# Sums placed where their exps end, keys loaded two gate steps sooner, last projection in column halves: sliding-window attention with a gated feed-forward block on one core

## The chip, the cores and the metric

The kernel runs on one core of a Trainium2 chip. The metric is the time of one execution in device microseconds. Every comparison below uses executions of the state "fast". The span of the trace is some 1.9 us shorter than that time (335.7 against 337.54 us in the profiled run of the kernel before); stretches of the trace are given in us from the start of the span.

Short names: PE is the tensor engine, DVE the vector engine, ACT the scalar engine, POOL and SP the two others. POOL, ACT and SP issue the transfers (DMA; POOLq, ACTq and SPq in the traces). PSUM is where the kernel keeps the tiles that PE writes (`o_ps`, `s_ps` and the like in the traces). In the traces `qT` and `kT` are the turned queries and keys, `xT` the output of the attention, `sg` the silu of a gate, `hT` the output of the gate steps and `wo` the output weights. A warming matmul is one whose result nobody reads. The fifth block of a projection is `c = 4`, the first that needs the second third of the output weights.

## The reference, cut to what matters

```python
def _attn_ref(q, k, v):                       # 8 batches, 8 heads, 576 rows, 64 columns
    scores = np.matmul(q, k.transpose(0, 1, 3, 2)) / np.sqrt(D)
    mask = (rel >= 0) & (rel < 64)            # rel = query row - key row
    attn = softmax(np.where(mask, scores, -1e9))
    return np.matmul(attn, v)

def _moe_ref(x, w_gate, w_val, w_out):        # x: 4608 x 512; 512 -> 1536 -> 512
    g = x @ w_gate
    return (g * sigmoid(g) * (x @ w_val)) @ w_out
```

The kernel cuts the 4608 rows into nine tiles of 512. A tile has four pairs of heads (scores, exp, sums of the exps, values), then twelve gate steps of eight 512-column matmuls, then a projection in four slices of twelve.

## The kernel before

The warming of PE at the start, while the first loads are under way:

```python
    nc.vector.memset(ones[:], 1.0)
    ...
    def keep_warm(n):
        for _ in range(n):
            nc.tensor.matmul(warm[0:D], ones[:, 0:D], ones[:])
    keep_warm(7)
```

The end of the first tile's attention. `totals` is the pair of matmuls for a pair's sums; the logarithm and an exp of its negative make the inverse.

```python
    def log_of(u):
        d_ps = one("d_ps")
        totals(0, u, d_ps)
        inverse[0, u] = room(1)[:, 0]
        log(inverse[0, u], d_ps)

    keep_warm(6)
    for u in range(2):
        values(0, u, ...)
    log_of(2)
    pairs = [gate_tiles() for _ in range(2)]
    gate_part(0, (0,), pairs, 0)
    log_of(3)
    gate_part(0, (1,), pairs[1:], 0)
    for u in (2, 3):
        invert(inverse[0, u])
    values(0, 2, one("ao_ps"))
    ...
```

The first tile's gate steps load and turn the second batch's keys, then turn its queries (a DVE transpose of data that POOL's queue loads):

```python
    for m in range(12):
        ...                                          # gate step m
        if 3 <= m < 7:                               # load two heads' keys, issued by ACT
            hs = slice(2 * m - 6, 2 * m - 4)
            load_runs(nc.scalar, raw_k[:, hs], k, 1, hs)
        if 7 <= m < 11:                              # cast them on ACT
            u = m - 7
            join(on_a, keys[:, u], raw_k[:, 2 * u:2 * u + 2])
        if m >= 8:                                   # transpose on PE, copy out on DVE
            u = m - 8
            ...
            split_k(kT[1][:, u, :], tp[:])
        if m >= 10:
            turn_q(1, m - 10)
    turn_q(1, 2)
    turn_q(1, 3)

    halves = out_tile(), out_tile()
    for u in range(4):
        scores(1, u)
        if u % 2:                                    # output weights: blocks 0-5, then 6-11
            project_part(0, (0, 1), halves, range(3 * u - 3, 3 * u + 3))
```

POOL's queue brings, in this order: the gate and value weights in ten transfers, the queries of batch 1 in four, the output weights in thirds of four blocks (`weights_o(0, 4)`, `(4, 8)`, `(8, 12)`), then v of batch 1. The last projection is four times `project`: twelve matmuls of 512 columns, one copy, four stores of 64 KB.

The softmax here doesn't subtract the row's maximum and nothing guards it: scores larger than these inputs give would overflow.

## Time and profile before

| | before |
|---|---|
| time, three runs | 337.47 us median (337.40 to 337.78) |
| span; PE busy | 335.7 us; 323.2 us (96%) |
| PE idle 21.3 to 42 us | 1.78 us |
| second batch's first gate matmul | 56.29 us |
| start of the last copy, and from there to the end | 331.26; 4.44 us |

How to read it: PE is the bound. Only its waits, and work that stands alone at the two ends, can be saved. The lines are in the prediction.

### The profile page before, as it was taken

The numbers are of one execution on the slowest core, as the hardware profiler recorded it, in microseconds if no ns is written. First come the engines' busy times: TensorE is split into PE (matmuls) and PEld (weight loads), VectorE is DVE, ScalarE is ACT, GpSimd is POOL, SyncE is SP. The second block draws the span as 40 slices with busy tenths as digits, with TensorE's granted clock in tenths as the row PEclk, the third lists the DMA queues.
The fourth block names the chain that finished last, engine by engine and source line by source line (L and its number), as shares of the span: only waits on it lengthen the run. The fifth ranks groups of instructions, "written<-read, shape, count | busy, mean of one in ns | idle before, by whom it ended". The sixth has DMA issues, their size and how long they took to land.

```text
span 335.7 us, 6932 instructions
## 1 busy us (share of the span) xinstructions
PE 323.2 (96%) x2683; PEld 153.9 (46%) x2729; DVE 214.2 (64%) x318; ACT 169.2 (50%) x241; POOL 137.8 (41%) x247
## 2 busy tenths in 40 slices
PE   8899799999999999999999999999999999999994
PEld 3444344444544454445444544444444444544441
DVE  5754766588667756785678656865786476753431
ACT  4764656336733763366435553565347633763300
POOL 5944345946767965256123896163200000000000
PEclk9999999999999999999999999999999999999999
DMA  7999999999899499639931999199401320010013
GB/s 261 205 202 226 229 188 223 125 205 215 147 248 186 52 176 234 124 58 209 185 89 20 170 180 167 12 189 177 111 0 48 79 56 3 23 72 31 3 32 94
DMA packets 83057, 44.12 MB, mean 131 GB/s; under 512 B 63824, under 2 KB 77648, under 8 KB 83024
## 3 DMA queue, kind: packets, MB, share of 16 engines
q0 software_dynamic: 49328, 22.56, 54.2%
q1 hardware_dynamic: 31680, 19.02, 20.6%
q10 hardware_dynamic: 2016, 2.10, 2.2%
q8 instruction: 21, 0.34, 0.4%
q14 instruction: 12, 0.10, 0.1%
HBM read 54.00 MB, written 9.44 MB: 189 GB/s over the span
## 4 chain that ended last, share of the span: by engine, by line
PE 88%; DMA 6%; DVE 3%; issue 2%; ACT 1%; DVEq 0%
PE g_ps L306 26%; PE v_ps L306 26%; PE o_ps L315 25%; PE s_ps L227 3%; DMA k_f<-in_k_dram 3%; PE ao_ps L271 3%; PE d_ps L245 3%; DMA q_f<-in_q_dram 1%; PE tp L174 1%; PE g_ps L286 1%; ACT E L233 1%; DVE kT L177 1%; PE v_ps L286 1%; DMA out_dram<-os__4409 1%; DMA out_dram<-os__4428 1%
## 5 line engine op out<-in xcount | busy, mean ns | idle before, releaser
L299 ACT ACTIVATE sg<-g_ps 128x512 f32<-128x512 f32 x108 | 64.4, 597 | 112.1 <-PE g_ps L306 79.9
L300 DVE TENSOR_TENSOR hT<-sg,v_ps 128x512 bf16<-128x512 f32 x108 | 74.9, 694 | 62.9 <-PE v_ps L306 59.9
L306 PE MATMUL v_ps<-xT,wv 128*128 128x512 bf16 x417 | 108.3, 379 | 0.5
L306 PE MATMUL g_ps<-xT,wg 128*128 128x512 bf16 x413 | 107.6, 379 | 0.5
L315 PE MATMUL o_ps<-wo,hT 128*128 128x512 bf16 x405 | 96.5, 380 | 1.6 <-issue 0.6
L107 POOL DMA_DIRECT2D k_s<-in_k_dram x112 | 60.7, 551 | 29.8 <-DMA q_s<-in_q_dram 20.5
L306 PEld LDWEIGHTS <-wv 128*128 128x128 bf16 x424 | 41.5, 98 | 50.0
L306 PEld LDWEIGHTS <-wg 128*128 128x128 bf16 x424 | 41.4, 98 | 49.5 <-issue 0.3
L315 PEld LDWEIGHTS <-hT 128*128 128x128 bf16 x432 | 39.6, 98 | 45.1 <-issue 0.4
L233 ACT ACTIVATE E<-s_ps 128x1024 bf16<-128x1024 f32 x36 | 35.2, 1021 | 8.4 <-PE s_ps L227 8.2
L277 DVE TENSOR_TENSOR xT<-ao_ps,r 128x512 bf16<-128x512 f32 x36 | 24.7, 691 | 22.7 <-ACT r L256 20.5
L196 DVE STREAM_TRANSPOSE kT<-k_s 128x512 bf16<-128x512 bf16 x28 | 35.9, 1284 | 0.0
L253 ACT ACTIVATE r<-d_ps 128x512 f32<-128x512 f32 (+1 forms) x35 | 21.0, 601 | 22.4 <-PE d_ps L245 22.4
L235 DVE TENSOR_TENSOR E<-E,mask 128x1024 bf16<-128x1024 bf16 x28 | 20.5, 739 | 11.5 <-ACT E L233 11.5
L87 POOL DMA_DIRECT2D q_s<-in_q_dram x28 | 15.3, 558 | 26.7 <-DVE qT L186 16.0
L148 POOL CAST v<-v_f 128x512 bf16<-128x512 f32 x22 | 14.3, 665 | 21.5 <-DMA v_f<-in_v_dram 17.5
L256 ACT ACTIVATE r<-r 128x512 f32<-128x512 f32 (+1 forms) x35 | 22.3, 641 | 1.1
L186 DVE STREAM_TRANSPOSE qT<-q_s 128x512 bf16<-128x512 bf16 x32 | 22.3, 702 | 0.0
L271 PEld LDWEIGHTS <-v 128*64 128x64 bf16 x576 | 13.8, 112 | 5.7 <-issue 1.7
L271 PE MATMUL ao_ps<-E,v 128*64 128x64 bf16 x576 | 15.3, 196 | 0.6 <-DVE v L156 0.6
L245 PE MATMUL d_ps<-E,ones 128*64 128x512 bf16 x72 | 13.9, 392 | 0.3
L227 PE MATMUL s_ps<-qT,kT 64*64 64x128 bf16 (+1 forms) x640 | 12.5, 211 | 0.2 <-DVE kT L177 0.2
(95 smaller groups left out, 175.6 us busy)
## 6 DMA issues: line engine op xcount, KB each, us to landing
q_s<-in_q_dram POOLq DMA_DIRECT2D x28, 248.0 KB, 6.7
k_s<-in_k_dram POOLq DMA_DIRECT2D x112, 56.0 KB, 5.2
v_f<-in_v_dram SPq DMA_DIRECT2D x22, 256.0 KB
v<-in_v_dram POOLq DMA_DIRECT2D x18, 128.0 KB, 4.8
k_f<-in_k_dram ACTq DMA_DIRECT2D x6, 256.0 KB
wo<-in_moe_w_out_dram POOLq DMA_DIRECT2D x3, 512.0 KB, 16.0
v<-v SPq DMA_DIRECT2D x6, 256.0 KB
v<-v SPq DMA_DIRECT2D x6, 192.0 KB
```

The lines of the kernel that those rows point to most:

```text
L107: nc.gpsimd.dma_start(k_s[p0:p0 + 32, g, :, 0:w], k[b, a:H:2, s:s + P].rearrange("u (r e) d -> r u (e d)", e=4) [:, :, 32 * c:32 * c + w],)
L186: nc.vector.transpose(queries[t][:, u, :].rearrange("r (e x) -> r e x", e=16), staged[t][0][:, u].rearrange("r (e d) -> r e d", d=D)[:, :, ...
L196: nc.vector.transpose(dst[:, u, :].rearrange("r (g x e) -> r g e x", g=4, e=4), k_s[:, :, u].rearrange("r g (e d) -> r g e d", d=D)[:, :, ...
L227: nc.tensor.matmul(blocks(s_ps[64 * c:64 * c + 64, h], t, lo, hi), zero[r] if src is None else src[r, u, x:x + 64], blocks(qT[r], t, lo, h ...
L233: nc.scalar.activation(E[:], s_ps[:], AF.Exp, scale=0.125)
L245: nc.tensor.matmul(d_ps[64 * h:64 * h + 64], ones[:, 0:D], weights[t, u][:, h, :])
L271: nc.tensor.matmul(blocks(o_ps[64 * h:64 * h + 64], t, m, m + 1), (v1, v2)[m // 4][t % 2][:, m % 4, 2 * u + h, :] if t == LAST else (v2, v ...
L277: nc.vector.tensor_mul(xT[t][:, u, :], o_ps[:], inverse.pop((t, u)))
L299: nc.scalar.activation(sg[:], g_ps[:], AF.Silu)
L300: nc.vector.tensor_mul(hT[t][:, m, :], sg[:], v_ps[:])
L306: nc.tensor.matmul(ps[:], w[:, c, P * m:P * m + P], xT[t][:, c, :], start=(c == 0), stop=(c == 3),)
L315: nc.tensor.matmul(o_ps[:], hT[t][:, c, P * s:P * s + P], wo[:, c, :], start=(c == 0), stop=(c == 11),)
```

## The change

The intent: put each sum on PE as soon as its exp has ended, so that logarithms and inverses are earlier; issue the second batch's keys two gate steps sooner, so that scores do not wait for them; and let half of the last output be copied and stored while PE computes the other half. PE's warming also starts after a quarter of the memset.

```diff
+    def project_last(t, s):
+        rows = out[S * batch(t):S * batch(t) + 512].rearrange("(r e) f -> e r f", e=16)
+        os_ = fsb.tile([P, 512], FP32, name="os_", tag="os_", bufs=3)
+        tiles = out_tile(), out_tile()
+        for x in range(2):
+            f = slice(256 * x, 256 * x + 256)
+            for c in range(12):
+                nc.tensor.matmul(
+                    tiles[x][:, 0:256], hT[t][:, c, P * s:P * s + P], wo[:, c, f],
+                    start=(c == 0), stop=(c == 11),
+                )
+            nc.vector.tensor_copy(os_[:, f], tiles[x][:, 0:256])
+            for i in range(4):
+                eng = nc.scalar if i % 2 else nc.sync
+                eng.dma_start(rows[4 * s + i][:, f], os_[32 * i:32 * i + 32, f])
@@ warming
-    nc.vector.memset(ones[:], 1.0)
+    nc.vector.memset(ones[:, 0:P], 1.0)
+    nc.vector.memset(ones[:, P:512], 1.0)
-    keep_warm(7)
+    for _ in range(6):
+        nc.tensor.matmul(warm[0:D, 0:P], ones[:, 0:D], ones[:, 0:P])
+    keep_warm(6)
@@ sums
-    keep_warm(6)
+    keep_warm(5)
+    log_of(2)
     for u in range(2):
         values(0, u, ...)
-    log_of(2)
+    log_of(3)
     pairs = [gate_tiles() for _ in range(2)]
-    gate_part(0, (0,), pairs, 0)
-    log_of(3)
-    gate_part(0, (1,), pairs[1:], 0)
+    gate_part(0, (0, 1), pairs, 0)
@@ keys
-        if 3 <= m < 7:          # loads, here with the slices moved alike
+        if 1 <= m < 5:
-        if 7 <= m < 11:         # casts
+        if 5 <= m < 9:
-        if m >= 8:              # transposes
+        if 6 <= m < 10:
-        if m >= 10:
-            turn_q(1, m - 10)
-    turn_q(1, 2)
+        if m >= 9:
+            turn_q(1, m - 9)
     turn_q(1, 3)
@@ tail
-    for s in range(4):
+    for s in range(3):
         project(NT - 1, s)
+    project_last(NT - 1, 3)
```

More of the change, by code (lines that the diff above doesn't have):

```diff
@@ L499 @@
             nc.vector.tensor_copy(mask[:, 1], mask[:, 0])
-        if 3 <= m < 7:
-            hs = slice(2 * m - 6, 2 * m - 4)
+        if 1 <= m < 5:
+            hs = slice(2 * m - 2, 2 * m)
             load_runs(nc.scalar, raw_k[:, hs], k, 1, hs)
-        if 7 <= m < 11:
-            u = m - 7
+        if 5 <= m < 9:
+            u = m - 5
             join(on_a, keys[:, u], raw_k[:, 2 * u:2 * u + 2])
-        if m >= 8:
-            u = m - 8
+        if 6 <= m < 10:
+            u = m - 6
             tp = ps_a.tile([P, 512], BF16, name="tp", tag="a")
```

## The prediction

> **What bounds the kernel now.** I read the page first, for the busy shares and the chain that ended last.
>
> ```profile
> span 335.7 us, 6932 instructions
> ...
> PE 323.2 (96%) x2683; PEld 153.9 (46%) x2729; DVE 214.2 (64%) x318; ACT 169.2 (50%) x241; POOL 137.8 (41%) x247
> ...
> PE 88%; DMA 6%; DVE 3%; issue 2%; ACT 1%; DVEq 0%
> ```
>
> The tensor engine (PE) is busy in 323.2 of 335.7 us, so at most 12.5 us are idle and only that, or matmul work itself, can be won. Where the idle time lies is in a table of busy time by stretch of the span (stretch, its length, then PE busy and instruction count, PEld, DVE, ACT, POOL, clock, DMA share, GB/s).
>
> ```profile
> 16.00:21.30 5.30, 4.94 (x50) 2.09 (x51) 2.13 (x5) 3.99 (x7) 3.31 (x6) 1.00 1.39 200
> 21.30:42.00 20.70, 18.92 (x112) 8.73 (x113) 12.84 (x25) 10.51 (x17) 7.25 (x10) 1.00 1.22 223
> ...
> 56.30:331.20 274.90, 272.01 (x2177) 129.15 (x2215) 178.12 (x245) 135.18 (x194) 108.59 (x195) 1.00 0.68 114
> 331.20:335.70 4.50, 0.03 (x1) 0.00 (x0) 0.69 (x1) 0.00 (x0) 0.00 (x0) 0.88 0.23 62
> ```
>
> From 56.3 to 331.2 PE is 99% busy and the waits list gives it no wait above 0.3 us: an earlier start of that stretch is passed on whole. What can be won lies before 42 us (1.78 us idle from 21.3 on) and in the last 4.5 us. The chain of waits and the timeline name the causes.
>
> ```profile
> 14.51 0.43 DVE v L156
> ...
> 16.76 0.34 PE d_ps L245 x2
> ...
> 29.26 9.63 DMA k_f<-in_k_dram
> ```
>
> ```profile
> 31.74 0.62 ACT L408 CAST k_b<-k_f 128x512 bf16<-128x512 f32 x1 [0.16 <-DMA k_f<-in_k_dram]
> ...
> 34.66 0.62 ACT L408 CAST k_b<-k_f 128x512 bf16<-128x512 f32 x1 [1.35 <-DMA k_f<-in_k_dram]
> ...
> 38.91 0.62 ACT L408 CAST k_b<-k_f 128x512 bf16<-128x512 f32 x1 [1.04 <-DMA k_f<-in_k_dram]
> ...
> 41.26 1.89 DVE L186 STREAM_TRANSPOSE qT<-q_s 128x512 bf16<-128x512 bf16 x3
> ...
> 42.02 0.22 PE L227 MATMUL s_ps<-qT,zero 64*64 64x64 bf16 x2 [1.66 <-DVE qT L186]
> ...
> 331.26 0.69 DVE L322 COPY os__4447<-o_ps 128x512 f32<-128x512 f32 x1 [1.90 <-DMA out_dram<-os__4428]
> ```
>
> The reader should see three places. The last key block of batch 1, issued at 29.26, is cast only at 38.91; its kT copy on DVE then stands before the query transposes, and PE waits 1.66 us for them at 42.02. A 0.34 us sum of pair 3 stands on the chain at 16.76. And after the last matmul (331.26) come a 0.69 us copy and some 3.7 us of storing with nothing beside them.
>
> [...] while the keys move (28 to 38 us) the table of queues counts 185 and 170 packets of the two queues from 28 to 30, and 251 and 253 from 36 to 38, and POOL's queue falls from about 205 to some 140 GB/s. [...] 7 warming matmuls take 3.20 us at 1.53, 6 take 1.48 us at 12.73. [...]
>
> **The change part by part.**
>
> *Warming.* The 128x512 memset takes 0.48 us. From 0.48 for 512 and 0.09 for the 32-element one, 128 columns take about 0.17, so PE starts near 1.2 instead of 1.53. Six matmuls of 128 columns and six of 512 take, at the slow 0.43 us per 512, 0.64 + 2.56 = 3.2 us: the same as before, so they end at 4.4, and the first transposes still wait for the cast that ends at 4.74. It pays only if the clock rises earlier. I count 0 to 0.1 us.
>
> *Sums of pairs 2 and 3.* Now ACT finishes the third pair's work at 12.0 and exp 3 at 15.11, but log 2 starts at 15.81 because its sums stand behind the values of pairs 0 and 1, and log 3 at 17.13. After the change sums 2 run near 14.0 while PE has to wait for the DVE copies of v anyway (end 14.94); log 2 starts at 15.15, sums 3 fill 15.35 to 15.7, log 3 is 15.85 to 16.45, and the two inversions (1.14) end at 17.6 instead of 18.77. The first gate matmul still waits for xT at 16.16. From there PE has 16 gate matmuls (3.45) and two groups of values (0.74), 4.2 us in all, and no sum; so it reaches 20.35 to 20.5 instead of 21.29. **Gain at gate step 2: 0.8 us.** The table load (1.28 us) moves with the inversions and ends at 18.9, before the first silu.
>
> *Keys.* They are issued at steps 1 to 4 instead of 3 to 6, that is 3.5 us plus the 0.8, near 20.4 to 24.9. In the kernel before, the first packet of the keys moved 3.4 us after its issue (none but 4 packets before 28 us). With the same delay they start near 23.9. Each DMA engine has 64 key packets of 59 ns, taken in turn with weight packets of 98 or 60 ns, so 20 x 157 + 44 x 119 ns = 8.4 us: all landed near 32.5, the first near 27. Casts now want them at steps 5 to 8, at 27.3, 29.1, 31.1 and 33: about in time, four steps from issue as before. The gate steps then run 20.45 + 10 x 1.727 + 4 transposes of 0.216 = 38.6, and scores 0 of batch 1 follow at once. Scores 1 need the second query transpose. The queries land near 36.6 (the POOL issue that waits for them leaves at 37.26, some 0.6 later), and the keys' earlier traffic delays this by the 14 or so packets still outstanding there, 0.8 us: 37.3. DVE then does transpose, hT, transpose, 0.7 each: 39.4. **Scores 1 go from 42.02 to 39.4, 2.6 us.**
>
> *What takes part of it back.* The projection after it starts at 39.9 instead of 42.38, and needs output weights that come last in POOL's queue. POOL's issues at 39.98, 42.55 and 45.06 wait for the first, second and third third of them, so these land near 39.4, 41.9 and 44.4. The byte total up to there is unchanged. The second third is now wanted at 39.9 + 8 x 0.216 = 41.6, and some 0.4 us go: c=4 starts at 42.0 instead of 44.1, **2.1 us**. The last third is wanted at about 44.4, just in time. The values' v shifts (49.57 before, some 47.5 after) find their data, the last of it near 48.2; batch 2's keys (landed near 62) are transposed at 66.43 now and 64.3 after. I see no further loss, and carry **2.0 to 2.1 us**.
>
> *Last projection.* 24 matmuls of 256 columns take what 12 of 512 did. The last copy is half as long: [...] The last four stores move 32 KB each in place of 64; their data take 332.8 to 333.9 now, of which I expect 0.1 to 0.2 to go. The issues (0.78 to 0.86 for two) and the 1.8 us from the last packet to the end stay. The first half is stored during the second half's matmuls. **Gain 0.4 us.**
>
> Sum: 0.05 + 2.05 + 0.4 = 2.5 us; 337.47 - 2.5 = **335.0**.
>
> **Rivals.** (a) The wait moves to the gate weights: the keys now share engines with the value weights of steps 6 to 9 (landed near 26). For it: those packets are delayed by 20 x 59 ns = 1.2 us. Against: they are wanted at 28.3. If the keys' start delay is longer, because the weight packets queued ahead are larger (98 ns, not 60), ACT stalls on the casts and PE up to 1.5 us: 336.3. (b) Everything before 45 us is bound by DMA: the DMA row of the page, 9 tenths in all slices from 8 to 126 us, speaks for it, PE with no DMA wait after 42 against. Then waits for output weights or queries take most of the 2.6 us, leaving 1 or less: 336.1 with the tail. (c) Output weights and queries come a little earlier than I read, all of 2.6 to 2.9 us is kept, and an earlier clock adds 0.3: 334.2. (d) DVE, now blocked at step 9 on the queries, holds back hT and so the gate's PSUM pair; PE has one step of slack, so I expect no cost, at most 0.5.
>
> **Range and chances.** Rivals (a) and (b) give the upper end with a margin, 336.3; (c) gives the lower, 334.1. A gain over 2% would need 6.7 us, about all the idle time outside the start; a loss of 2% a new wait of 7 us. Faster 0.01, within 2% 0.985, slower 0.005.
>
> **What would show it.** The first gate step of the second kind (g_ps, 21.29 now) at 20.3 to 20.7; casts of k_b near 27.3, 29, 31 and 33 with waits under 0.5; a wait of DVE's first qT transpose on queries near 37; scores 1 at 39 to 40; a PE wait on output weights near 41.6; the second batch's gates (56.3 now) near 54.2; the last matmul about 2.1 us earlier and 4.1 in place of 4.5 us after it. The prediction fails if the key casts come later than 34, if a gate step waits for weights, or if the lead at 45 us is not found at 56.

The sum came to 0.05 + 2.05 + 0.4 = 2.5 us, that is 335.0. Of the 0.4 for the last projection, the term for the shorter copy, 0.27 us, is cut, as it was worked out with a rate that no trace shows; the 0.1 to 0.2 for the stores stay, and with them alone the terms come to 2.2 to 2.3 us. That packets of two queues are taken in turn is the reading of the packet counts (185 and 170, 251 and 253).

## The result and the profile after

The changed kernel takes **335.39 us** (median of four runs, 335.31 to 335.77), the kernel before 337.62 (four runs, 337.40 to 338.62). The ratio is 0.993, with a 95% interval of 0.9909 to 0.9952. A ratio here is the mean time of one kernel's fast runs over that of the other's of the same rounds, so it is not quite the ratio of the medians quoted. The class is "within 2%", and 335.39 lies in the predicted range of 334.1 to 336.3, 0.4 us above the forecast of 335.0.

The page of the changed kernel, its span, busy times and the chain by engine:

```profile
span 333.5 us, 6973 instructions
...
PE 322.6 (97%) x2700; PEld 155.2 (47%) x2745; DVE 213.7 (64%) x320; ACT 169.0 (51%) x241; POOL 138.5 (42%) x247
...
PE 84%; DMA 9%; POOL 3%; issue 1%; ACT 1%; DVE 0%; SPq 0%; POOLq 0%
```

Of the 2.2 us, 1.6 are idle time of PE (12.5 before, 10.9 now) and 0.6 are busy time. The busy time went before gate step 2, where PE is busy for 17.59 us instead of 18.25: one warming matmul is gone, and in this pair of traces the clock rose at 4.67 instead of 6.94 us (the first eight transposes took 0.62 instead of 1.03 us). DMA's part of the chain has grown from 6% to 9% although the kernel became faster. The table of busy time by stretch (columns as in the prediction) places the time:

```profile
20.50:40.00 19.50, 19.00 (x131) 9.18 (x132) 12.61 (x24) 9.81 (x17) 7.20 (x10) 1.00 1.22 224
40.00:54.90 14.90, 13.95 (x154) 6.50 (x158) 10.57 (x21) 9.77 (x13) 5.50 (x11) 1.00 1.48 213
...
329.90:333.50 3.60, 0.00 (x0) 0.00 (x0) 0.40 (x1) 0.00 (x0) 0.00 (x0) 0.84 0.25 72
```

In the stretch of the gate steps only 0.5 us are idle (1.78 before), but in the next there are 0.95, against 0.3 in the comparable one before. The tail is 3.6 instead of 4.5 us. The timeline of the changed kernel (start, length, engine, line, operation, tiles; in brackets the idle time before and what ended it) shows the mechanism:

```profile
27.26 0.61 ACT L427 CAST k_b<-k_f 128x512 bf16<-128x512 f32 x1
...
32.89 0.61 ACT L427 CAST k_b<-k_f 128x512 bf16<-128x512 f32 x1
...
37.60 0.71 DVE L186 STREAM_TRANSPOSE qT<-q_s 128x512 bf16<-128x512 bf16 x1 [0.61 <-DMA q_s<-in_q_dram]
...
39.56 0.22 PE L227 MATMUL s_ps<-qT,zero 64*64 64x64 bf16 x2 [0.36 <-DVE qT L186]
...
42.56 1.02 PE L315 MATMUL o_ps<-wo,hT 128*128 128x512 bf16 x4 [0.67 <-DMA wo<-in_moe_w_out_dram]
...
329.88 0.42 DVE L355 COPY os__4439<-o_ps 128x256 f32<-128x256 f32 x1 [0.89 <-PE o_ps L351]
```

The casts no longer wait. DVE now waits for the queries, and PE, which reaches the projection 2.4 us sooner (39.99 instead of 42.38), waits 0.67 us for output weights. The chain of waits says the same in one line each:

```profile
15.06 12.88 DMA wv<-in_moe_w_val_dram
27.94 0.28 issue
28.22 14.30 DMA wo<-in_moe_w_out_dram
42.52 0.04 issue
42.56 1.02 PE o_ps L315 x4
```

From 15.06 to 42.5 us the chain is one of transfers; where before it ran through a key block, it runs now through weights in POOL's queue. From there on nothing waits long (PE's longest single wait after 43 us is 0.2 us): the second batch's gates begin at 54.88 (56.29 before), 1.41 us sooner. The last copy starts at 329.88 (331.26), 1.38 us sooner, and the rest, 2.19 - 1.38 = 0.81 us, comes after it.

### The profile page after: what moved, and what is told of

The parts are those of the page before. It is cut to its first block, busy times and chain, and to the rows that moved or that the text cites. A ratio compares the mean times of both kernels' runs of the same rounds, so it can differ in the third digit from the quotient of the medians.

```text
span 333.5 us, 6973 instructions
## 1 busy us (share of the span) xinstructions
PE 322.6 (97%) x2700; PEld 155.2 (47%) x2745; DVE 213.7 (64%) x320; ACT 169.0 (51%) x241; POOL 138.5 (42%) x247
## 4 chain that ended last, share of the span: by engine, by line
PE 84%; DMA 9%; POOL 3%; issue 1%; ACT 1%; DVE 0%; SPq 0%; POOLq 0%
PE o_ps L315 26%; PE v_ps L306 25%; PE g_ps L306 25%; DMA wo<-in_moe_w_out_dram 4%; DMA wv<-in_moe_w_val_dram 4%; PE d_ps L245 3%; PE s_ps L227 3%; PE ao_ps L271 2%; DMA q_f<-in_q_dram 1%; POOL wg L160 1%; PE o_ps L351 1%; POOL wv L160 1%; ACT E L233 1%; POOL v L128 1%; POOL v L148 0%
## 5 line engine op out<-in xcount | busy, mean ns | idle before, releaser
L315 PE MATMUL o_ps<-wo,hT 128*128 128x512 bf16 x394 | 94.3, 380 | 2.3 <-DMA wo<-in_moe_w_out_dram 0.7
L315 PEld LDWEIGHTS <-hT 128*128 128x128 bf16 x420 | 38.4, 98 | 44.7 <-issue 1.6
```

The source lines that it names most:

```text
L315: nc.tensor.matmul(o_ps[:], hT[t][:, c, P * s:P * s + P], wo[:, c, :], start=(c == 0), stop=(c == 11),)
```

## The experiments

**Theory of bytes.** After the change, what PE waits for up to 45 us are transfers that come in a fixed order at the rate of the DMA engines (224 GB/s from 20.5 to 40 us); so the earlier steps' leads are lost, and the front gain is set by the landing of the output weights. **Rival, additive parts.** Each part hands its own lead on to the end. For the tail, the question was whether 0.8 us belong to it or only the 0.4 predicted.

Twelve runs followed, all with correct results (after_again is the changed kernel itself). The first four share one chip and seven runs of the kernel before (337.56 us median), the other eight another chip with seven or eight (337.43, 337.42).

| run | parts in it | time, us | ratio to before |
|---|---|---|---|
| tail_only | tail | 337.60 (two clocks, see below) | 0.9992 |
| keys_only | keys | 336.45 | 0.9957 |
| no_warm | sums, keys, tail | 335.52 | 0.9933 |
| no_sums | warming, keys, tail | 335.45 | 0.9928 |
| no_keys | warming, sums, tail | 336.13 | 0.9952 |
| keys_tail | keys, tail | 335.70 | 0.9945 |
| after_again | all | 335.80 | 0.9944 |
| after_extra | all, and 256 KB more | 336.91 | 0.9986 |
| before_extra | none, and 256 KB more | 337.72 | 1.0006 |
| gap_filled | none, filler matmuls | 337.23 | 0.9993 |
| three_parts | all, projection in three parts | 335.53 | 0.9945 |
| three_parts_b | the same, last part slice by slice | 335.32 | 0.9936 |

The 95% intervals reach 0.13 to 0.3% to either side, 0.4 to 1 us; so differences of a few tenths rest on the traces, not on the times. Each run has one trace, and traces differ too: in the two of the changed kernel the second batch's gates start at 54.88 and 55.48.

### The parts undone or alone

The edits are pieces of the diff above. For `no_sums`, for instance:

```diff
-    keep_warm(5)
-    log_of(2)
+    keep_warm(6)
     for u in range(2):
         values(0, u, ...)
-    log_of(3)
+    log_of(2)
     pairs = [gate_tiles() for _ in range(2)]
-    gate_part(0, (0, 1), pairs, 0)
+    gate_part(0, (0,), pairs, 0)
+    log_of(3)
+    gate_part(0, (1,), pairs[1:], 0)
```

and for `no_warm`:

```diff
-    nc.vector.memset(ones[:, 0:P], 1.0)
-    nc.vector.memset(ones[:, P:512], 1.0)
+    nc.vector.memset(ones[:], 1.0)
-    for _ in range(6):
-        nc.tensor.matmul(warm[0:D, 0:P], ones[:, 0:D], ones[:, 0:P])
-    keep_warm(6)
+    keep_warm(7)
```

> The kernel before with only the keys (and the transposes after them) two steps sooner. Theory of bytes: what starts the projection's fifth block is the landing of the second third of the output weights, near 42.4 us whatever came earlier; so keys alone bring the whole front gain, 1.3 to 1.5 us (fifth block near 42.5, against 44.1), though gate step 2 stays at 21.3. Rival, each part adds its own: keys alone bring 1.4 less the 0.76 that gate step 2 gained, about 0.6.

Measured: 336.45 us, 1.1 below the kernel before; the second batch's gates at 55.11, 1.18 sooner. Its timeline:

```profile
40.18 1.90 PE L315 MATMUL o_ps<-wo,hT 128*128 128x512 bf16 x8
42.54 1.02 PE L315 MATMUL o_ps<-wo,hT 128*128 128x512 bf16 x4 [0.46 <-DMA wo<-in_moe_w_out_dram]
```

The fifth block starts at 42.54, as in the full change (42.56): the same landing decides. The gain lies below the 1.3 to 1.5 of the theory and well above the rival's 0.6.

> The changed kernel with the old warming (one memset of 512, seven matmuls of 512). Clock up again near 6.9 us (4.7 in the changed kernel) and the first gate matmul near 15.9 to 16.2 instead of 15.26, if the earlier clock comes from the warming[...]. Theory of bytes: the time stays within 0.2 us of the changed kernel, since the second gate matmul waits for a weight load until 16.05, the queries until 37.6 and the output weights until 42.5. Rival, the lead is handed on: 0.6 to 0.9 us slower than the changed kernel.

Measured: 335.52, against 335.39 for the full change. It was run at another time. So undoing the warming costs some 0.1 us, less than the interval resolves, as the theory of bytes has it. The fifth block waits until 42.74 for its weights.

> The changed kernel with the sums of pairs 2 and 3 at their old places (and six warming matmuls before the values). Gate step 2 near 20.5 to 21.2 instead of 20.53. Theory of bytes: the second third of the output weights still decides, fifth block near 42.5, time within 0.2 us of the changed kernel. Rival, the 0.8 us that I gave to the sums are handed on: 0.5 to 0.8 us slower than the changed kernel.

Measured: 335.45. Here too nothing is lost at the end (one of four runs, the one with the trace, took 336.25, the other three 335.31 to 335.51), and the fifth block waits until 42.95.

> The kernel before with the keys sooner and the split last projection, without the new warming and the sums' new places. Each of those two was worth 0.1 us when undone alone. Theory of bytes: both together are worth no more than 0.3 us, 335.5 to 335.7 us. Rival, each covers for the other (a lead of 0.6 us from either is enough): 336.0 or more.

Measured: 335.70, against 335.80 for the full change. Warming and sums together are worth nothing that could be measured, once the keys come sooner. The additive rival in its size of 0.76 us falls; a few tenths could hide in the intervals, but the fifth block starts at 42.80 here and at 42.79 in after_again, so the same landing decides in both.

> The changed kernel once more, for the comparison on the same chip with the other three of this call: 335.3 to 335.6 us.

Measured: 335.80, slightly above the expectation, with runs from 335.29 to 336.04. In its trace the first gate matmul starts at 15.98 (15.26 in the first trace of the same kernel), and the fifth block at 42.79. The first trace was thus an early one, and 1.41 us is at the upper end of what the front gains: over the traces without a half clock the second batch's first silu starts at 57.36, 57.24 and 57.04 without any of the front parts (the kernel before, before_extra and gap_filled), and at 55.94 and 56.55 with all, 57.2 and 56.25 on average, which is 1.0 us.

> The changed kernel with the keys and their transposes at their old steps: warming, sums and tail remain. Then nothing waits for the output weights (fifth block of the projection later than 42.5) and the casts of the keys decide as before. If the lead at gate step 2 (0.76 us) moves the keys' issue and landing with it: scores 1 near 41.2, second batch's gates near 55.5, and with the tail's 0.7 some 1.5 us less than before, 336.0. If the keys land when the bytes ahead of them allow: the tail alone, some 0.7 less, 336.8. In both a wait of 1.7 us before scores 1, which in some executions may bring a half clock for 3.4 us and 1.2 us more, as in two of four of the run with the tail alone.

Measured: 336.13 us, 1.3 below. The second batch's gates start at 55.72. The casts wait for keys again, 0.91, 1.36 and 1.02 us, and PE 1.7 us before scores 1, at 41.45; no output weight is waited for. So without the keys the lead of the sums (with the warming, from which this run doesn't part it) does reach the end, 0.4 to 0.6 us of it, which with the tail's 0.8 makes the 1.3. The first of the two expected outcomes is nearer.

### The tail

> The kernel before with only the last projection in two column halves. The trace of the changed kernel has 3.7 us from the last matmul to the end, against 4.5 before: 0.8 us, twice the 0.4 that I predicted. If this belongs to the split, the last matmul stands as before (within 0.1 of 331.2 us after the span's start) and the time falls by 0.7 to 0.9 us (ratio 0.9975). If only the shorter copy and issue belong to it and the rest was chance in the landing of the last store, it falls by 0.4.

Measured: 338.16, 336.87, 337.05 and 338.19 us. The two quick ones are 0.5 to 0.7 below the kernel before, where 0.7 to 0.9 were expected; the slow ones have a mean granted clock of 0.995 and 0.994 instead of 0.998 and 1.000. The profile fell on a slow one, so the last matmul ends later than expected, at 332.64 (331.23 before). But what follows the start of the last copy lasts 336.33 - 332.68 = 3.65 us, as in the full change (3.64), against 4.44 before. The other runs agree: keys_only, before_extra and gap_filled, without the split, have 4.43 to 4.44; all ten with it have 3.64 to 3.71. The 0.8 us belong to the split, then. They consist of the copy, 0.69 to 0.42 (0.27); the time from the copy's end to the end of the last packet, 2.05 to 1.76 (0.29), of which 0.8 pass before the first packet in the kernel before (331.98 to 332.79); and from there to the end of the span, 1.71 to 1.46 (0.24), with packets of 2 KB and of 1 KB. The last piece I had not expected; in the runs with the split it is 1.46 to 1.53, in those without it 1.69 to 1.71, so it is not chance. And keys_only and keys_tail, which differ by the split, are 1.11 and 1.72 below the kernel before, which gives 0.6.

### A transfer added

```diff
+    spare = cst.tile([P, 2, DM], BF16, name="spare")
+    nc.gpsimd.dma_start(
+        spare[:], moe_w_out[0:2 * P].rearrange("(c r) f -> r c f", r=P)
+    )
     weights_o(0, 4)
```

> The changed kernel with one more transfer, 256 KB of output weights into a tile that nobody reads, ahead of the output weights in the same queue. It costs each DMA engine 16 packets of 98 ns, 1.6 us. Theory of bytes: the projection's fifth block waits until 44.1 instead of 42.56 and the time grows by 1.3 to 1.6 us. Rival (tensor engine or DVE order decides, DMA has room): 0 to 0.3.

Measured: 336.91, 1.1 above after_again and 1.5 above the first result. PE's timeline:

```profile
41.47 1.90 PE L315 MATMUL o_ps<-wo,hT 128*128 128x512 bf16 x8 [1.32 <-DMA wo<-in_moe_w_out_dram]
43.98 1.02 PE L315 MATMUL o_ps<-wo,hT 128*128 128x512 bf16 x4 [0.61 <-DMA wo<-in_moe_w_out_dram]
```

The fifth block comes at 43.98, where 44.1 was expected; now the first third is waited for too.

> The kernel before with the same added transfer. There the fifth block starts at 44.1, 1.7 us after its weights landed, so by the theory of bytes the transfer costs nearly nothing: 0 to 0.4 us. If bytes bound the kernel before too (rival), 1.3 to 1.6 us as in the changed one.

Measured: 337.72, 0.3 above the kernel before, with an interval of the ratio (0.9991 to 1.0021) that includes no change:

```profile
41.90 0.22 PE L227 MATMUL s_ps<-qT,zero 64*64 64x64 bf16 x2 [1.36 <-DVE qT L186]
...
42.26 2.76 PE L315 MATMUL o_ps<-wo,hT 128*128 128x512 bf16 x12
```

The same bytes cost 1.1 to 1.5 us in one kernel and about 0.3 in the other. This is the test that tells the theories apart: before the change the output weights had room at this point and the keys decided; after it, the weights decide. That the kernel before was bound by the bytes of this queue here, the rival of this run, falls. Nor is it a late issue that decides in the changed kernel: the second third was issued at 28.22, long before the first third landed at 39.94, so the queue was not empty between; and DMA moves 224 GB/s from 20.5 to 40 us, against 223 from 21.3 to 42 before the change.

### The half clock

The trace of tail_only shows a clock of one half for one stretch. The table by stretch, cut at 42.66 and 46.07 us, between which its clock is 0.50, and as much, 3.41 us, before:

```profile
39.25:42.66 3.41, 1.67 (x43) 1.10 (x44) 3.19 (x6) 3.25 (x4) 0.56 (x2) 1.00 1.25 209
42.66:46.07 3.41, 3.41 (x10) 1.22 (x8) 1.38 (x3) 0.57 (x1) 1.07 (x2) 0.50 2.11 169
```

A window is here such a stretch of 3.41 us. That windows follow one another at this length is the estimate from the clock records: in the kernel before, the clock is 1.00 from 6.94 to 334.62 us and then 0.50, in the changed one 1.00 from 4.67 to 332.35, both 327.68 us or 96 times 3.413; the windows of the other traces are laid off in the same way (6.94 + 9 x 3.413 = 37.66 in the kernel before). PE was busy for 1.67 of 3.41 us in one window, because the whole 1.69 us wait before scores 1 fell into it, and it ran at half the clock in the next: twelve projection matmuls took 4.45 us there instead of 2.76. In no_keys, whose wait also fell into one such window, PE was busy for 1.72 of 3.41 us and kept its clock:

```profile
39.19:42.60 3.41, 1.72 (x44) 1.02 (x42) 3.18 (x7) 3.25 (x4) 0.70 (x2) 1.00 1.24 207
```

In the kernel before, the profiled run had the wait divided over two windows (2.67 and 2.40 busy). Its run of 339.10 us had a mean clock of 0.992; it has no trace, so that it was of this kind is likely but not shown. That a wait which falls whole into one window brings the half clock was the guess from these traces. To test it:

```diff
+    filler = ps_f.tile([P, 512], FP32, name="filler", tag="v")
     for u in range(4):
         scores(1, u)
+        if u == 0:
+            for _ in range(7):
+                nc.tensor.matmul(filler[0:D], ones[:, 0:D], ones[:])
```

> The kernel before with seven idle matmuls of 512 columns (1.5 us) between scores 0 and scores 1 of batch 1, where the tensor engine waits 1.7 us. If the half clock of some executions comes from that wait[...], none of these executions is slow (mean clock 0.996 or more, none above 338.2 us) and the others stand within 0.2 us of the kernel before. If it has another cause, one in five or so is slow as with the kernel before.

Measured: six runs of 337.01 to 337.60, clock 0.998 or more, none slow. But the eight runs of the kernel before that go with it had none above 338.08 either (clock 0.996 to 0.998). So this is in line with the guess and does not show it. Nor does PE's busy time in a window decide alone: 1.67 us was followed by the half clock and 1.72 was not, but in the window around the last matmul 1.36 us (no_keys, 329.32 to 332.74) was followed by it and 1.41 (gap_filled, 329.50 to 332.91) was not. What else counts stays open.

### Can the new wait be filled?

```diff
         if u % 2:
-            project_part(0, (0, 1), halves, range(3 * u - 3, 3 * u + 3))
-    for s in range(2):
-        project_end(0, s, halves[s])
+            project_part(0, (0, 1), halves, range(2 * u - 2, 2 * u + 2))
     ...
     for u in range(2):
         sums(1, u, d_tile())
+    project_part(0, (0, 1), halves, range(8, 12))
+    for s in range(2):
+        project_end(0, s, halves[s])
```

(The sums of pairs 0 and 1 and the loads for batch 2 move before the last part, the v shifts after the two output copies.)

> The changed kernel with the first projection in three parts, blocks 0 to 3, 4 to 7 and 8 to 11, with scores 2 and 3 and the sums of pairs 0 and 1 between them, and the v shifts after the output copies. Correct result. Theory of bytes: the weights land no sooner (second third near 42.5, third near 45.1), but scores and sums fill the two waits, so the second batch's gates start near 54.2 instead of 54.88 and the time falls by 0.5 to 0.8 us, to about 334.7. Rival: the wait of 0.67 us only moves to the last third or to the v data (landed near 48.4): within 0.2 us of the changed kernel.

Measured: 335.53 us, no gain. Two waits took the place of the one:

```profile
45.36 1.89 PE L315 MATMUL o_ps<-wo,hT 128*128 128x512 bf16 x8 [0.55 <-DMA wo<-in_moe_w_out_dram]
47.81 2.75 PE L315 MATMUL o_ps<-wo,hT 128*128 128x512 bf16 x12 [0.56 <-DVE os__796 L322]
```

The first is the last third of the weights, the second a PSUM buffer whose copy could only start when both slices had ended. The rival expectation was right in the outcome. In three_parts_b the last part runs slice by slice:

```diff
-    project_part(0, (0, 1), halves, range(8, 12))
     for s in range(2):
+        project_part(0, (s,), (halves[s],), range(8, 12))
         project_end(0, s, halves[s])
```

> The projection in three parts again, but its last part slice by slice, so that the first slice's copy runs beside the second slice's matmuls. In the first form the tensor engine waited 0.55 us for the last third of the output weights at 45.36 and 0.56 us for the copy at 47.81. If the second was only the order, it goes: projection of slice 2 near 47.25, second batch's gates near 54.5, 0.3 to 0.5 us below the changed kernel of this call. If the v data or another copy takes its place: no difference.

Measured: 335.32 us, six runs: 334.94, 335.00, 334.94, 336.20, 335.64, 335.65; after_again 335.80. The second batch's gates start at 54.29, sooner than in any other trace, and both waits are gone:

```profile
45.19 4.56 PE L315 MATMUL o_ps<-wo,hT 128*128 128x512 bf16 x20
```

It has the three lowest times of all, 334.94 twice and 335.00, and the lowest median, but 0.9936 and 0.9944 with intervals of some 0.0015 to each side overlap: the gain of 0.3 to 0.5 us is seen in the trace, which is of one of the two quickest runs, and not shown by the times.

## Why the prediction was right or wrong

The time and the class were right: 2.5 us were forecast and 2.2 measured. The front term was mis-sized upwards and the tail downwards, and that the total came close is partly luck.

- **Warming, 0 to 0.1 us: right.** The clock rose at 4.67 instead of 6.94 us in the first pair of traces and the first gate matmul came 0.9 us sooner, which looked like a gain. Over all traces it was not: the first gate matmul starts at 15.21 to 16.16 with the old warming (seven traces, mean 15.56) and at 15.26 to 16.19 with the new (seven, mean 15.70). The clock rises at 4.31 to 7.00 us with the old and at 3.82 to 5.75 with the new, so the change may bring it forward, but nothing that follows needs it.
- **Sums, 0.8 us at gate step 2: the 0.76 of the first trace is luck, and the term was about double the average.** In that trace the lead was there before the sums: the first gate matmul, forecast at 16.16 as before, came at 15.26. From it to gate step 2 PE then took 5.27 us, where the working has 4.2 (the kernel before took 5.13). The failing step is "4.2 us in all": it adds up the times of the matmuls alone, where the kernel before takes 4.79 for them without its sum. To take the one sum, 0.34 us, off the measured 5.13 would have forecast a gain of 0.34. The silu of step 2 starts at 22.14 on average in seven traces with the sums at their old places, and at 21.72 in the seven with the new: 0.42 us. The working also left out that the first value weights can come later than the first gate matmul: in the changed kernel PE waited 0.41 us for them at 16.05. That this lead is worth nothing at the end, where the keys come sooner, the prediction did not say; it counted it within the 2.6.
- **Keys: right in its main steps up to scores 1.** Casts were forecast at 27.3, 29.1, 31.1 and 33, and were at 27.26, 28.99, 30.94 and 32.89; the keys' first packet moved at 23.88 (23.9), 3.6 us after its issue at 20.32 (in the kernel before it was 3.8 us, 24.08 to 27.86, where the working has 3.4); the wait of DVE for queries ended at 37.60 (37.3); scores 1 were at 39.56 (39.4). The last key packet moved at 31.35, sooner than the 32.5 forecast, which changed nothing.
- **What takes part of it back: the right mechanism, the wrong size.** The failing step is "so these land near 39.4, 41.9 and 44.4", read as 0.6 us before POOL's issues. The 0.6 came from the queries, but the trace puts POOL's issue at 37.26 down to DVE's kT copy and not to their landing. In the kernel before, the second third landed at 42.27, only 0.28 us before POOL's issue at 42.55; in the changed kernel it landed at 42.52 (28.22 + 14.30). In all seven traces where PE waits for this third, PE starts 0.24 us before POOL's issue (42.56 and 42.80, 42.54 and 42.78, 42.79 and 43.03, for instance). So the wait was 0.67 instead of 0.4 and the fifth block started at 42.56 instead of 42.0. The last third was not "just in time" everywhere: four traces (keys_only, no_warm, no_sums, after_again) wait 0.24 to 0.47 us for it. The front lead was 1.4 us in the first trace and 1.0 on average, not 2.05. This is rival (b), in part. The added transfer confirms it. (The DMA row of the page is at 9 tenths from 8 to 84 us; up to 126 us, where the rival has 9 throughout, it then reads 8, 9, 9, 4 and 9.)
- **Rivals (a) and (d)**: apart from the 0.41 us at 16.05 no gate step waited for its weights, and DVE's wait for queries cost PE 0.36 us, inside the limit of 0.5.
- **Tail, 0.4 us: too small by half.** The copy took 0.42 instead of 0.69 us, 0.27 less, which is what the cut term had; 24 matmuls of 256 columns took 2.63 us, where 12 of 512 took 2.60. "Their data, of which I expect 0.1 to 0.2 to go" were 0.29 with the issue, and "the 1.8 us from the last packet to the end stay" was wrong: 1.71 became 1.46.

What stays open: why the closing of smaller stores is quicker, what brings the half clock, and how often it meets the kernel before.

## What to carry to other kernels

Before you add up the leads of several edits, ask for each following wait when its data land, in the order of the queue: a lead that arrives before that landing is lost in the wait (with the keys moved and nothing added, the fifth block waited and started at 42.54 to 42.95 in six traces, whichever other parts were in). To forecast what an edit leaves of a stretch, take what it removes off the measured length of the stretch; a sum of the parts that remain came out 0.6 us too short here. Read a landing from the engine that waits for it, not from the next issue (0.24 us later here), and check a gain seen in one pair of traces against the spread of several. Splitting the last output in two paid here at both its copy (0.27 us) and its stores (0.53), with nothing after it in which the gain could be lost: 0.8 us in the traces, of which the times show 0.5 to 0.7.
